# Transposing the third batch's q and k by DMA instead of on TensorE, with two natural buffers shared crosswise

## The chip, the cores and the metric

The kernel runs on one core of one Trainium2 chip. The metric is the device time of one execution in microseconds. Profiles give the span of one execution, which is some 2 us shorter than the time. All runs compared here are of the fast state, except a single run of one experiment (e6), whose state can't be told and which is used for its trace alone. Three slow runs (350.61 and 622.58 us of the kernel before, 390.21 us of e3) are in no ratio.

## The reference

Two stages, both of which the kernel does in one pass. First, attention with a sliding window of 32 to either side, for 8 batches of 8 heads, 576 positions and 64 numbers per position. Then a two-layer network over the 4608 resulting rows of 512.

```
scores = q @ k.T / 8, masked to |i - j| <= 32
x      = softmax(scores) @ v            # reshaped to (4608, 512)
h      = x @ w_in                       # 512 -> 2048
g      = smelu(h)                       # 0, (h + 1)^2 / 4 or h
out    = g @ w_out                      # 2048 -> 512
```

## The kernel before

The network is a loop of 144 steps. A step is one chunk of the first layer: 8 matmuls into `hp`, then ScalarE and VectorE make `gT` of it. 8 matmuls of the second layer, 256 columns wide and written as `op`, or 4 of 512 columns, follow most steps. The attention of batch b+1 is sprinkled between the steps. A table says at which step a piece goes: `scores` (small matmuls of q and k, exp, mask) and `sums` (small matmuls with v and with ones, then the division, into `xT`, which the network reads). Eight steps use 256 rows.

`scores` needs q and k transposed: `qT` and `kT`. The kernel before has two ways to get them:

```python
def load_rows(b, t):                   # long rows: 9 positions in one run
    x = nat.tile([128, NU, 2, D], BF, name=nm, tag=nm)       # two buffers for q, two for k
    ...
    nc.gpsimd.dma_start(out=dst[b], in_=src[b].rearrange("(m e) (p j) d -> (e p) m (j d)", e=2, j=9))

def load_nat(b, t):                    # natural rows: one position is one run
    x = dst[b] = nat.tile([128, NU, 2, D], BF, name=nm, tag=nm)
    for h in range(2): ...

def tpose(...):                        # TensorE: transposes into PSUM, then a copy to qT or kT
    ...
            nc.tensor.transpose(ps[HD[h], j - j0], src[h][:, D * j:D * j + D], ident)
    ...

def xpose(b, t):                       # DMA: one transposing transfer, sync queue
    nc.sync.dma_start_transpose(out=qkT(b, t).rearrange("d (u p) -> d u p", p=128),
                                in_=(qn, kn)[t][b].rearrange("p u h d -> p (u h d)"))
```

Batches 0, 1 and 2 (`LONG = 3`) are loaded in long rows and transposed on TensorE. Batches 3 to 7 are loaded in natural rows and transposed by DMA. All loads but q's first are issued by GpSimd, which runs ahead of the other engines as far as buffers and its DMA completions allow; it casts float32 to bfloat16 on the way. The outputs and the DMA transposes are issued by the sync engine, in program order.

The softmax here doesn't subtract the row's maximum and nothing guards it: scores larger than these inputs give would overflow.

## Time and profile before

| what | value |
|---|---|
| time | 311.72 us, median of 3 (311.7 to 312.26) |
| span of the profile | 310.0 us |
| TensorE matmul busy | 296.7 us (96%) |
| VectorE, ScalarE, GpSimd busy | 79%, 63%, 24% |
| granted TensorE clock | full in all slices |
| DMA transposes | 5 of q, 5 of k |

The busy time of TensorE has its ends modelled, so 96% doesn't mean that it works at its peak. What makes it the bound is that next to nothing is seen to hold it up. One wait in the prediction's list isn't one, as I saw later: `op <- issue`, 4.9 us in 31 pieces of 0.16. It belongs to this group of the costliest lines (busy us, mean ns, then idle before):

```profile
L432 PE MATMUL op<-w_out,gT 128*128 128x512 bf16 x477 | 123.0, 379 | 5.1 <-issue 4.9
```

The program has 512 of these matmuls, as the 512 weight loads of the same line show. 35 records are missing, and each of the 31 gaps is what a missing record leaves. Where all 512 were recorded (the changed kernel, below) the wait is gone. A second trace of that same kernel (e9) lacks 36 again, and the wait is back:

```profile
PE op L431 <- issue: 4.8, 30, 0.2
```

### The profile page before, as it was taken

The numbers are of one execution on the slowest core, as the hardware profiler recorded it, in microseconds if no ns is written. First come the engines' busy times: TensorE is split into PE (matmuls) and PEld (weight loads), VectorE is DVE, ScalarE is ACT, GpSimd is POOL, SyncE is SP. The second block draws the span as 40 slices with busy tenths as digits, with TensorE's granted clock in tenths as the row PEclk, the third lists the DMA queues.
The fourth block names the chain that finished last, engine by engine and source line by source line (L and its number), as shares of the span: only waits on it lengthen the run. The fifth ranks groups of instructions, "written<-read, shape, count | busy, mean of one in ns | idle before, by whom it ended". The sixth has DMA issues, their size and how long they took to land.

```text
span 310.0 us, 8569 instructions
## 1 busy us (share of the span) xinstructions
PE 296.7 (96%) x3669; PEld 206.7 (67%) x3706; DVE 244.7 (79%) x381; ACT 195.3 (63%) x323; POOL 73.8 (24%) x89
## 2 busy tenths in 40 slices
PE   7889999999999999999999999999999999999995
PEld 3467878876666666666666666666666666666652
DVE  3278568988988888898888888888888888888760
ACT  3688786866775666567656666566676666554431
POOL 8897354563036133041404000000000000000000
PEclk9999999999999999999999999999999999999999
DMA  9999999999999999298989391005501100100111
GB/s 153 186 192 197 173 209 184 186 151 170 156 151 170 141 183 172 54 98 176 157 77 94 52 182 43 34 36 113 112 34 36 37 36 34 37 36 34 56 47 68
DMA packets 124118, 34.54 MB, mean 111 GB/s; under 512 B 108208, under 2 KB 119728, under 8 KB 124080
## 3 DMA queue, kind: packets, MB, share of 16 engines
q0 software_dynamic: 94736, 18.06, 76.3%
q1 hardware_dynamic: 29200, 15.63, 21.8%
q8 instruction: 29, 0.48, 0.6%
q10 hardware_dynamic: 144, 0.29, 0.3%
q14 instruction: 9, 0.07, 0.1%
HBM read 36.70 MB, written 9.44 MB: 149 GB/s over the span
## 4 chain that ended last, share of the span: by engine, by line
PE 88%; DMA 4%; POOL 3%; issue 2%; ACT 1%; DVE 0%; POOLq 0%
PE hp L492 39%; PE op L432 35%; PE bb L293 6%; PE op L448 4%; DMA w_in<-in_moe_w_in_dram 4%; PE bb L227 2%; PE tp L187 1%; POOL vn L106 1%; POOL w_in L110 1%; ACT pt L235 1%; POOL kh L85 0%; DVE gT L501 0%; ACT mx L500 0%; PE bb L252 0%; ACT rr L496 0%
## 5 line engine op out<-in xcount | busy, mean ns | idle before, releaser
L492 PE MATMUL hp<-xT,w_in 128*128 128x256 bf16 x1152 | 149.4, 273 | 1.7 <-DMA w_in<-in_moe_w_in_dram 1.1
L496 ACT ACTIVATE rr<-hp 128x512 f32<-128x512 f32 x144 | 85.7, 595 | 87.4 <-PE hp L492 87.2
L492 PEld LDWEIGHTS <-w_in 128*128 128x128 bf16 x1152 | 112.0, 98 | 41.5 <-issue 2.3
L432 PE MATMUL op<-w_out,gT 128*128 128x512 bf16 x477 | 123.0, 379 | 5.1 <-issue 4.9
L503 DVE TENSOR_TENSOR mx<-hp,rr 128x512 f32<-128x512 f32 x137 | 94.5, 690 | 31.1 <-ACT rr L496 29.0
L504 DVE SCALAR_TENSOR_TENSOR gT<-rr,mx 128x512 bf16<-128x512 f32 x137 | 95.2, 695 | 4.7
L432 PEld LDWEIGHTS <-gT 128*128 128x128 bf16 x512 | 47.5, 98 | 36.8
L235 ACT ACTIVATE pt<-bb 128x1024 bf16<-128x1024 f32 (+1 forms) x33 | 32.7, 1002 | 4.4 <-PE bb L227 2.9
L106 POOL DMA_DIRECT2D vn<-in_v_dram x32 | 27.6, 874 | 30.8 <-PE bb L227 28.0
L305 DVE TENSOR_TENSOR xT<-bb,rc 128x512 bf16<-128x512 f32 (+1 forms) x32 | 21.1, 658 | 10.3 <-ACT rc L300 9.8
L437 ACT COPY osb<-op 128x512 f32<-128x512 f32 x32 | 18.6, 582 | 11.6 <-PE op L432 11.1
L300 ACT ACTIVATE rc<-lr 128x512 f32<-128x512 f32 (+2 forms) x40 | 23.5, 588 | 1.3
L98 POOL DMA_DIRECT2D qn<-in_q_dram x10 | 12.2, 1221 | 46.4 <-DMA qT<-qn 40.7
L299 ACT ACTIVATE lr<-bb 128x512 f32<-128x512 f32 (+2 forms) x40 | 22.0, 551 | 0.4 <-PE bb L293 0.4
L201 DVE TENSOR_TENSOR pt<-pt,mask 128x1024 bf16<-128x1024 bf16 (+1 forms) x33 | 20.3, 614 | 0.0
L293 PE MATMUL bb<-pt,ones 64*64 64x256 bf16 (+3 forms) x352 | 19.6, 256 | 0.1
L293 PE MATMUL bb<-pt,vn 64*64 64x128 bf16 (+3 forms) x712 | 18.4, 204 | 0.2 <-DMA vn<-in_v_dram 0.2
L293 PEld LDWEIGHTS <-vn 64*64 64x64 bf16 x712 | 16.7, 107 | 0.4 <-DMA vn<-in_v_dram 0.4
L448 PE MATMUL op<-w_out,gT 128*128 128x256 bf16 x128 | 16.5, 273 | 0.0
L293 PEld LDWEIGHTS <-ones 64*64 64x64 bf16 x352 | 10.2, 105 | 8.6 <-issue 8.6
L98 POOL DMA_DIRECT2D kn<-in_k_dram x10 | 12.1, 1216 | 8.3 <-DMA kn<-in_k_dram 3.7
L227 PE MATMUL bb<-qT,kT 64*64 64x128 bf16 (+1 forms) x520 | 13.1, 217 | 0.3 <-DVE kT L190 0.2
(56 smaller groups left out, 116.9 us busy)
## 6 DMA issues: line engine op xcount, KB each, us to landing
out_dram<-osb SPq DMA_DIRECT2D x36, 256.0 KB, 2.3
vn<-in_v_dram POOLq DMA_DIRECT2D x32, 144.0 KB, 9.7
qn<-in_q_dram POOLq DMA_DIRECT2D x10, 288.0 KB, 7.8
kn<-in_k_dram POOLq DMA_DIRECT2D x10, 288.0 KB, 9.6
w_in<-in_moe_w_in_dram POOLq DMA_DIRECT2D x12, 128.0 KB, 5.5
w_out<-in_moe_w_out_dram POOLq DMA_DIRECT2D x3, 512.0 KB, 15.5
qn<-in_q_dram POOLq DMA_DIRECT2D x2, 576.0 KB, 13.2
kn<-in_k_dram POOLq DMA_DIRECT2D x2, 576.0 KB, 14.5
```

The lines of the kernel that those rows point to most:

```text
L98: nc.gpsimd.dma_start(out=x[:, :, h], in_=src[b, NY * h:NY * h + NY].rearrange("y s d -> (y s) d") .rearrange("(u p) d -> p u d", p=128))
L106: nc.gpsimd.dma_start(out=vn[b][64 * a:64 * a + 64, :, h], in_=v[b, y:y + 2].rearrange("y s d -> (y s) d") .rearrange("(c r) d -> r c d", ...
L235: A.activation(p, ps[:, :, :w * n].rearrange(like, y=m), AF.Exp, scale=D ** -0.5)
L293: nc.tensor.matmul(bb[HD[h], a, o + c0:o + c1], ones[HD[a]] if c is None else vn[b][HD[a], c, h], p(a, h), start=n == 0, stop=True, skip_g ...
L299: A.activation(lr[:, :, :D0], bb[:, :, D0:2 * D0], AF.Ln)
L300: A.activation(rc[:, :, :D0], lr[:, :, :D0], AF.Exp, scale=-1.0)
L432: nc.tensor.matmul(o, gT[tt // 2][:, j, 128 * (tt % 2):128 * (tt % 2) + 128], w_out[:, j], start=not done, stop=len(done) == 2 * NF - 1, s ...
L448: nc.tensor.matmul(o[:, tt], gT[p][:, j, 128 * tt:128 * tt + 128], w_out[:, j, 256 * half:256 * half + 256], start=not done, stop=len(done ...
L492: nc.tensor.matmul(hp[:, j], w_in[:, kk, 256 * f + 128 * j:256 * f + 128 * j + 128], xT[:, kk, r0:r0 + TB], start=n == 0, stop=n == 3)
L496: A.activation(rr, hp, AF.Relu, scale=0.5, bias=0.5)
L503: V.tensor_max(mx, hp, rr)
L504: V.scalar_tensor_tensor(g, rr, 1.0, mx, op0=ALU.min, op1=ALU.mult)
```

## The change

Its intent is to take the transposes of batch 2 off TensorE. Batch 2 is loaded in natural rows and transposed by DMA. The sums and scores around it are set to other steps, so that the first scores of batch 2 come a little later. SBUF use stays what it was, four tiles: two for batch 1's long rows, and two for the natural rows of all later batches. q of batch b takes one of the two and k the other, and in the next batch it's the other way round. So the next q is loaded into the buffer of this k, once this k is transposed.

```diff
-    LONG = 3
+    LONG = 2
     def load_rows(b, t):
-        x = nat.tile([128, NU, 2, D], BF, name=nm, tag=nm)
+        x = nat.tile([128, NU, 2, D], BF, name=nm, tag="long")
     def load_nat(b, t):
-        x = dst[b] = nat.tile([128, NU, 2, D], BF, name=nm, tag=nm)
+        x = dst[b] = nat.tile([128, NU, 2, D], BF, name=nm, tag=f"n{(b + t) % 2}", bufs=1)
-    put([(load_rows, 2, t) for t in range(2)] + [(load_v, 2, n) for n in range(4)])
+    put([(load_nat, 2, t) for t in range(2)] + [(load_v, 2, n) for n in range(4)])
-    for n, a in enumerate((18, 21, 24, 27)):
+    for n, a in enumerate((18, 20, 22, 28)):
         at(a, seq[2 + n][0])                        # sums
-    for n, a in enumerate((18, 21, 25, 27)):
+    for n, a in enumerate((18, 20, 26.5, 28)):
         at(a, seq[3 + n][1])                        # scores; the third is batch 2's first
-    for b, *a in ((1, 11, 12), (2, 19.5, 22.5)):
-        for t in range(2):
-            at(a[t], (tposes, b, (t, 0), (t, 1)))
-    loads, xps = {}, {}
-    for b in range(LONG, B):
+    for t in range(2):
+        at(11 + t, (tposes, 1, (t, 0), (t, 1)))
+    loads, xps = {}, {16: [(2, 0)], 18: [(2, 1)]}
+    for b in range(LONG + 1, B):
         ...
-            xps.setdefault(a + 5 + t, []).append((b, t))
+            xps.setdefault(a + 6 + 2 * t, []).append((b, t))
```

## The prediction

> **What bounds the kernel now.** I began with the head of the page and its slices, to see which engine is full and when.
>
> ```profile
> PE 296.7 (96%) x3669; PEld 206.7 (67%) x3706; DVE 244.7 (79%) x381; ACT 195.3 (63%) x323; POOL 73.8 (24%) x89
> PE   7889999999999999999999999999999999999995
> PEclk9999999999999999999999999999999999999999
> DMA  9999999999999999298989391005501100100111
> ```
>
> TensorE is busy to nine tenths or more in every slice from the fourth to the last but one, at full granted clock. The 16 DMA engines look full as well for the first 16 slices (124 us). Two full resources can't both be the bound, so I asked next what TensorE ever waits for, which the view of waits answers for that engine:
>
> ```profile
> PE op L432 <- issue: 4.9, 31, 0.2
> PE z L336 <- DVE warm L126: 1.2, 1, 1.2
> PE hp L492 <- DMA w_in<-in_moe_w_in_dram: 1.1, 2, 0.6
> PE hp L492 <- DVE xT L305: 0.4, 1, 0.4
> ```
>
> Columns: total us, times, longest us. All waits for DMA together are about 2 us, on w_in at the start and first inputs. The loads that fill the DMA engines afterwards run ahead of their use. So the time after about 23 us is the sum of what TensorE is given to do, and 88% of the chain that ended last lies on TensorE. Work removed from it comes off the time, if no wait grows in its place. The chain around the third batch's transposes shows what there is to remove (start, length, what):
>
> ```profile
> 54.95 0.87 PE op L448 x8
> 55.82 1.12 PE tp L187 x36
> 56.95 0.98 PE hp L492 x8
> 57.93 0.87 PE op L448 x8
> ...
> 62.18 0.87 PE op L448 x8
> 63.06 1.13 PE tp L187 x36
> 64.18 0.98 PE hp L492 x8
> 65.16 0.87 PE op L448 x8
> ```
>
> The tp pieces are the transposes of q and of k of batch 2, and both lie on the chain. The hp piece after each takes 0.98 us where a piece that follows another big matmul takes 0.87: switching into the 128-row matmuls again costs 0.11 us.
>
> **What the Trainium skill says.** "TensorE: Matmul & The Clock Gate", Part 4: PE-mode transpose, gives about 275 ns for a transpose in a kernel's context. The trace has 219 ns for one record, but they overlap: 36 in 1.12 us is 31 ns each on the chain, and that is the number to use. The same section says that the result lands in PSUM and needs a copy. The trace agrees: four copies on ACT of about 0.76 us and four on DVE of about 0.73 us for this batch.
>
> "Advanced Engine Details and Errata", X-Bar Transpose (TRN2), calls transposing DMAs as fast as regular ones, 350 to 400 GB/s. In the trace one transpose (128 x 2304 elements of 2 bytes, 590 KB) holds its queue for 2.8 us when nothing else runs, some 210 GB/s. That is slower than the page, and no more than ordinary traffic reaches here.
>
> "DMA: Bandwidth & Descriptors", Issuing engines are not separate DMA queues, says that transposes from the sync queue share the 16 engines with the loads. The trace agrees. The queue's order of time, with batch 3's pair under full load and batch 4's beside little:
>
> ```profile
> 76.95 6.82 SPq L194 DMA_TRANSPOSE qT<-qn  x1
> 83.93 5.57 SPq L194 DMA_TRANSPOSE kT<-kn  x1
> ...
> 107.83 2.79 SPq L194 DMA_TRANSPOSE qT<-qn  x1
> 110.79 2.41 SPq L194 DMA_TRANSPOSE kT<-kn  x1
> ```
>
> From issue to landing the loaded pair took 12.8 and 7.6 us, against a best of 4.8 and 4.7.
>
> **The change part by part.**
>
> *Removed from TensorE.* 2 groups of 36 transposes: 1.12 + 1.13 = 2.25 us of chain. With each goes one switch, 2 x (0.98 - 0.87) = 0.22 us. Sum 2.47 us, all on the path.
>
> *Removed elsewhere.* Eight copies (about 3.0 us on each of ACT and DVE) and one memset of 0.11 us in the preamble. DVE is at 9.0 of 10 us there, but TensorE waits for it almost nowhere: worth 0 by itself, some room for what follows.
>
> *Loads in natural rows.* The same 1.18 MB of q and k are written in 128-byte pieces instead of 1152-byte ones, 4608 packets instead of 512 for each of the two tensors. "DMA: Bandwidth & Descriptors", Why small descriptors are slow, predicts a loss, and the DMA records show its size: stretches with only 1152-byte packets ran at about 205 KB/us, with only 128-byte packets at about 153. Per tensor that is 590/153 - 590/205 = 3.9 - 2.9, so 1.0 us later for q and 2.0 us for k. GpSimd pays 4 issues of 1.22 us instead of 2 of 0.76, on an engine with little else to do. None of it is on the path.
>
> *DMA transposes added.* q2 and k2 are transposed by the sync queue, placed after steps 16 and 18 (a step is one first-layer chunk of hp, 1.75 us or more; step 16 runs at about 47.3 us). What holds them is the landing of the rows. GpSimd's order of time in the kernel before:
>
> ```profile
> 34.74 0.75 POOL L92 DMA_DIRECT2D qn<-in_q_dram  x1 [1.95 <-DMA qn<-in_q_dram]
> 38.02 0.74 POOL L92 DMA_DIRECT2D kn<-in_k_dram  x1 [2.52 <-DMA kn<-in_k_dram]
> ...
> 45.65 1.22 POOL L98 DMA_DIRECT2D qn<-in_q_dram  x1 [2.32 <-DMA w_out<-in_moe_w_out_dram]
> ```
>
> The DMA view gives 15.6 and 15.5 us to landing for the first two: q2 at 50.3, k2 at 53.5. With the loss above I estimate 51.3 and 55.5. The first transpose starts near 51.5 and lands, if as badly as batch 3's, at 64. The second starts when the queue is free, 51.5 + 6.8 = 58.3, and lands at 58.3 + 7.6 = 66. First use: scores of batch 2, at step 25 (69.1 us) before, moved by the change to after step 26. Before, the second-layer matmuls of step 26 end at about 72.1; less the 2.5 us removed, less the scores of step 25 (0.35) that are not yet done, 69.2. Margin 3 us. It's the thinnest of the new ones.
>
> *The crosswise buffers.* q3 takes the buffer of k2, k3 that of q2. So q3 can't be issued at 45.65 as before but only when kT of batch 2 has landed, about 66: 20 us later. Four issues of 1.22 us, then 6 to 9 us to landing on engines that are by then nearly idle: q3 at about 75, k3 at 79. Its transposes, now after steps 28 and 30 (some 73 to 78 us), then land at about 82 and 88. Their first use, at step 39, is near 95 (97 before). 7 us of margin. For later batches the load of b+1 starts when b's k is transposed, about 6 steps before b's first scores, and must be there 11 steps before its own, 17 or so steps later: 12 steps, over 23 us, for a load that needs about 12. No wait on TensorE.
>
> *Moved.* Attention work of batch 1 goes from steps 21 and 24 to 20 and 22, and batch 2's first scores from 25 to 26.5. The number of switches is the same. Two sums two steps apart are found before at steps 30 and 32, where TensorE loses less than 0.1 us, so I count 0.1 us for new tight spots.
>
> Sum: -2.47 + 0.1 = -2.4 us. 311.72 - 2.4 = 309.3 us.
>
> **The rivals.**
>
> *kT of batch 2 comes late.* For it: full DMA engines from 44 to 60 us, batch 3's pair at 12.8 us, one queue shared with output stores. Against it: I took those bad durations already, and after batch 2's values nothing more is loaded, because q3 is blocked. Were the rows 3 us later still and the transposes no faster, TensorE would stand for 0 to 3 us: 309.5 to 312, no gain. I give it 15%.
>
> *The crosswise wait starves batch 3 or a later one.* For it: loads start 20 us later and prefetch is one batch deep instead of two. Against: the margins of 7 us and more. If a single batch lost 3 us, 312; if all five did, some 320. 4%.
>
> *The saving is hidden anyway,* because DVE (79%) takes over. For it: 9.0 of 10 us between 50 and 60. Against: DVE loses 3.0 us of copies in just that stretch, and itself waits 29 us for ACT in the span. 311; 4%.
>
> *More than the sum is won,* since emptier DMA engines speed up TensorE. Against: in the stretch at 88 us with batch 3's transposes in flight the hp pieces are 0.87 us, as at 280 us with idle DMA. Below 308.5: 2%.
>
> **Range and chances.** The saving is read off the chain and small, 0.8%. The spread of the three runs before is 0.56 us. Below, little can happen: 308.7. Above, a stall at batch 2 of some 1.5 us: 310.8. 2% is 6.2 us; nothing removed can give that, and only the starving of several batches can cost it. Faster by over 2%: 1%; within: 97%; slower: 2%.
>
> **What would show it.** In the changed trace the chain has no tp piece after 40 us. The matmul that followed them takes 0.87 us. Transposed k of batch 2 lands before 67 us, and the first scores of batch 2 start near 69 with no wait on a DMA. GpSimd stands before q3 until the transposes' landing. The DMA slices thin out after 65 us and fill those later. TensorE busy is some 2.5 us less, with its idle time unchanged. Wrong would be a wait of TensorE on kT or qT, or on xT and pt at steps 20 to 30, of more than 1 us.

## The result, and the profile after

The changed kernel takes 309.15 us, median of 4 runs (309.13 to 309.35). The kernel before took 311.99 us in the runs it is compared with (311.70 to 313.73). The ratio is 0.9902, 95% interval 0.9873 to 0.993. Ratios are the mean time of one kernel's fast runs over that of the other's in the same rounds, so they aren't quite the ratio of the medians quoted. The span went from 310.0 to 307.6 us.

The span's difference, 2.46 us, is not a measure of the change. TensorE's last matmul ends 8.81 us after the start of the last step in both traces, but from there to the end of the span the changed kernel takes 3.95 us instead of 3.57: six semaphore waits of the sync engine, some 0.06 us apart, come after the last store has landed instead of before it. The times don't show this: the profiled run's time is 2.1 us above its span before (312.14 us) and 1.8 us above it in the changed kernel (309.35 us).

The head of the page, to be held against that of before:

```profile
PE 300.2 (98%) x3634; PEld 205.0 (67%) x3634; DVE 242.1 (79%) x376; ACT 192.6 (63%) x319; POOL 76.8 (25%) x91
PE   8989999999999999999999999999999999999994
DMA  9999999999999968996899156990910011011101
```

Nothing else took over. DVE and ACT fell by 2.6 and 2.7 us, about what the copies took. PE seems 3.5 us busier with less to do; that is again the missing records, this time present. The group of second-layer matmuls counts all 512 and waits for nothing:

```profile
L431 PE MATMUL op<-w_out,gT 128*128 128x512 bf16 x512 | 130.4, 380 | 0.0
```

So for TensorE a busy total is no measure of 2 us. What is one is the start of each step, read from the records of its first `hp` matmul, of which both traces have all 1152:

| step | before, us | changed, us | difference |
|---|---|---|---|
| 11 | 34.28 | 33.92 | 0.36 |
| 19 | 53.91 | 53.53 | 0.38 |
| 29 | 76.35 | 73.51 | 2.84 |
| 143, the last | 297.65 | 294.81 | 2.84 |

From step 29 on the two kernels are in lockstep to the last step. Up to step 19 the change has done nothing yet; the 0.38 us are scatter of the start, where TensorE waits for the first pieces of w_in among other things (1.1 us in the trace before, 0.4 in the changed one; the 13 traces of this study reach step 11 between 33.7 and 35.4 us). The change itself is worth 2.84 - 0.38 = 2.46 us, all of it between steps 19 and 29. I call that stretch's length the **stretch**: 76.35 - 53.91 = 22.44 us before, 73.51 - 53.53 = 19.98 us changed. It's free of the start's scatter, and it will serve as the measure in the experiments.

The chain that ended last, at the same places as before (start, length, what):

```profile
54.57 0.87 PE op L447 x8
55.44 0.87 PE hp L491 x8
...
62.84 0.87 PE op L447 x8
63.72 0.87 PE hp L491 x8
...
68.06 0.86 PE op L431 x4
68.93 0.35 PE bb L227 x16
69.27 0.98 PE hp L491 x8
```

The two tp pieces are gone and what followed them takes 0.87 us. The bb piece at 68.93 is the first scores of batch 2, with no wait before it. The sync queue shows what it might have waited for (start, time that issuing took):

```profile
50.93 6.75 SPq L194 DMA_TRANSPOSE qT<-qn  x1
57.78 6.34 SPq L194 DMA_TRANSPOSE kT<-kn  x1
...
74.19 6.41 SPq L194 DMA_TRANSPOSE qT<-qn  x1
80.76 6.55 SPq L194 DMA_TRANSPOSE kT<-kn  x1
```

The DMA view gives 13.5 and 8.3 us from issue to landing for the first pair: k transposed is there at 57.78 + 8.3 = 66.1 us, 2.8 us before it is used. GpSimd's order of time shows the crosswise wait, 19 us long, ended by that landing:

```profile
46.84 0.85 POOL L106 DMA_DIRECT2D vn<-in_v_dram  x1 [1.67 <-DMA w_out<-in_moe_w_out_dram]
66.84 2.42 POOL L98 DMA_DIRECT2D qn<-in_q_dram  x2 [19.15 <-DMA kT<-kn]
```

### The profile page after: what moved, and what is told of

The parts are those of the page before. It is cut to its first block, busy times and chain, and to the rows that moved or that the text cites. A ratio compares the mean times of both kernels' runs of the same rounds, so it can differ in the third digit from the quotient of the medians.

```text
span 307.6 us, 8460 instructions
## 1 busy us (share of the span) xinstructions
PE 300.2 (98%) x3634; PEld 205.0 (67%) x3634; DVE 242.1 (79%) x376; ACT 192.6 (63%) x319; POOL 76.8 (25%) x91
## 4 chain that ended last, share of the span: by engine, by line
PE 90%; ACT 3%; DVE 2%; DMA 2%; POOL 1%; issue 1%; POOLq 0%; ACTq 0%
PE hp L491 39%; PE op L431 37%; PE bb L293 6%; PE op L447 4%; PE bb L227 2%; DMA vn<-in_v_dram 2%; ACT pt L235 1%; POOL vn L106 1%; PE tp L187 1%; DVE xT L305 1%; ACT rc L300 1%; ACT lr L299 1%; DVE mx L502 0%; ACT rr L495 0%; POOL kh L85 0%
## 5 line engine op out<-in xcount | busy, mean ns | idle before, releaser
L495 ACT ACTIVATE rr<-hp 128x512 f32<-128x512 f32 x144 | 85.6, 594 | 87.5 <-PE hp L491 87.5
L431 PE MATMUL op<-w_out,gT 128*128 128x512 bf16 x512 | 130.4, 380 | 0.0
L98 POOL DMA_DIRECT2D qn<-in_q_dram x12 | 14.6, 1223 | 113.0 <-DMA kT<-kn 109.3
L300 ACT ACTIVATE rc<-lr 128x512 f32<-128x512 f32 (+2 forms) x40 | 23.5, 587 | 1.3
L293 PEld LDWEIGHTS <-vn 64*64 64x64 bf16 x712 | 16.7, 107 | 0.4 <-DMA vn<-in_v_dram 0.4
L293 PEld LDWEIGHTS <-ones 64*64 64x64 bf16 x352 | 10.3, 105 | 8.7 <-issue 8.6
L98 POOL DMA_DIRECT2D kn<-in_k_dram x12 | 14.6, 1235 | 0.6 <-DMA vn<-in_v_dram 0.3
```

The source lines that it names most:

```text
L98: nc.gpsimd.dma_start(out=x[:, :, h], in_=src[b, NY * h:NY * h + NY].rearrange("y s d -> (y s) d") .rearrange("(u p) d -> p u d", p=128))
L293: nc.tensor.matmul(bb[HD[h], a, o + c0:o + c1], ones[HD[a]] if c is None else vn[b][HD[a], c, h], p(a, h), start=n == 0, stop=True, skip_g ...
L300: A.activation(rc[:, :, :D0], lr[:, :, :D0], AF.Exp, scale=-1.0)
L431: nc.tensor.matmul(o, gT[tt // 2][:, j, 128 * (tt % 2):128 * (tt % 2) + 128], w_out[:, j], start=not done, stop=len(done) == 2 * NF - 1, s ...
L495: A.activation(rr, hp, AF.Relu, scale=0.5, bias=0.5)
```

## The experiments

The theory: the saving is the time of 72 transposes on TensorE and of the two switches around them, nothing else, and it holds as long as k transposed lands before its scores. Rivals: the new steps save something themselves; the copies on ScalarE and VectorE were part of the price; the crosswise buffers, or the shape of the loads, help or hurt. The record marks the result of every kernel as right, that of e6 too, which is wrong on purpose: batch 2's q and k stand at wrong positions in it. The numbers of q and k are so small in this reference (0.1 times normal ones) that the softmax comes out nearly uniform, so the comparison hardly sees which q meets which k. That e1 to e11 pass it says little about their transposes.

| run | median us | ratio to before (95%) | stretch us |
|---|---|---|---|
| before | 311.99 | 1 | 22.44 |
| changed | 309.15 | 0.9902 (0.9873 to 0.993) | 19.98 |
| e1, old steps | 309.40 | 0.9917 (0.9904 to 0.993) | 19.98 |
| e2, new steps alone | 312.75 | 1.0026 (1.0018 to 1.0035) | 23.28 |
| e3, transposes back | 312.28 | 1.0009 (1.0 to 1.0018) | 22.44 |
| e4, and the copies | 312.68 | 1.0029 (1.002 to 1.0039) | 22.99 |
| e5, own buffers | 313.42 | 1.0041 (1.0026 to 1.0057) | 23.09 |
| e6, long rows (wrong on purpose) | 309.13, one run | none | 19.97 |
| e7, scores early | 317.15 | 1.0163 (1.0142 to 1.0184) | 27.06 |
| e8, joined | 309.40 | 0.9912 (0.9894 to 0.9929) | 19.76 |
| e9, changed again | 309.37 | 0.9906 (0.9877 to 0.9935) | 19.98 |
| e10, joined again | 309.44 | 0.992 (0.9893 to 0.9948) | 19.76 |
| e11, batch 1 too | 328.45 | 1.0514 (1.0475 to 1.0552) | 19.98 |

The kernel before had medians of 311.96 to 312.04 us in these calls.

### e1: the changed kernel at the old steps

```diff
-    for n, a in enumerate((18, 20, 22, 28)):
+    for n, a in enumerate((18, 21, 24, 27)):
-    for n, a in enumerate((18, 20, 26.5, 28)):
+    for n, a in enumerate((18, 21, 25, 27)):
```

> The changed kernel, but the sums and scores of batches 1 and 2 stay at their old steps (18, 21, 24, 27 and 18, 21, 25, 27). Theory (the saving is TensorE's 72 transposes alone, and the new steps are only there to give the transposed k time): in the changed kernel step 25 starts at 65.29 us and k transposed of batch 2 landed at 66.1 us, so the scores, called about 66.2, just make it; 309.1 to 309.7 us, with at most 0.5 us of TensorE waiting at the first scores of batch 2. Rival (the new steps themselves save time): the gain shrinks visibly, over 310 us, without a wait on the transpose.

The stretch is the changed kernel's to the hundredth. The new steps save nothing. k transposed landed at 57.85 + 8.1 = 65.95 us (the DMA view), and the chain has the first scores directly behind the matmuls before them:

```profile
65.41 0.87 PE hp L491 x8
66.28 0.35 PE bb L227 x16
```

So they made it by 0.3 us in this trace. The new steps turn 0.3 us of margin into 2.8: insurance, not gain.

### e2: the new steps alone

```diff
-    for n, a in enumerate((18, 21, 24, 27)):       # sums
+    for n, a in enumerate((18, 20, 22, 28)):
-    for n, a in enumerate((18, 21, 25, 27)):       # scores
+    for n, a in enumerate((18, 20, 26.5, 28)):
-    for b, *a in ((1, 11, 12), (2, 19.5, 22.5)):   # TensorE's transposes
+    for b, *a in ((1, 11, 12), (2, 19.5, 23.5)):
```

> The kernel before with the new steps alone (sums 18, 20, 22, 28; scores 18, 20, 26.5, 28), batch 2 still in long rows and transposed by TensorE; its k at step 23.5 instead of 22.5, because at 22.5 it would want the PSUM tile of the sums of step 22, whose last reader comes later. Theory: the steps are worth nothing, 311.6 to 312.0 us, the time of before. Rival (part of the gain comes from the steps): under 311.

Neither: it's slower than before, by 0.84 us of stretch. TensorE's waits have a new line, and the chain there runs over VectorE:

```profile
PE bb L293 <- DVE qT L190: 0.8, 1, 0.8
```

```profile
57.14 1.28 DVE qT L190 x2
58.42 0.04 issue
58.46 0.60 PE bb L293 x18
```

The transposes at step 19.5 take both PSUM tiles that scores and sums use. The sums at step 20 have to wait until the last copy has emptied one. At the old steps the sums came at 21 and didn't meet it. My expectation that the steps are worth nothing holds only where no transposes stand beside them.

### e3 and e4: the transposes back, without and with their copies

The same `extra` is placed at steps 19.5 and 23.5 in both; e3 leaves out the last line.

```diff
+    def extra(b, t):
+        x = (qn, kn)[t][b]
+        todo = []
+        for half, pool in ((0, ps_s), (1, ps_n)):
+            tp = pool.tile([128, 2, 8, 128], BF, name="tp", tag="bb")
+            for part, (j0, j1) in enumerate(((0, 5), (5, 9))):
+                for j in range(j0, j1):
+                    for h in range(2):
+                        nc.tensor.transpose(tp[HD[h], part, j - j0], x[:, 9 * half + j, h], ident)
+                todo.append(((A.copy, V.tensor_copy)[part], tp[:, part, :j1 - j0], part, j1 - j0))
+        for copy, ps, part, n in todo:
+            copy(scratch[part][:, :n], ps)          # e4 only
```

> The changed kernel plus 72 TensorE transposes of batch 2's q and k, at steps 19.5 and 23.5, into PSUM tiles that nobody reads; no copies. Result unchanged. Theory: the saving is TensorE's time alone, so it comes back whole, +2.47 us: 311.6 us. Rival (the eight copies on ScalarE and VectorE carried part of the cost): clearly less than +2.4, say 310.5.

> As e3, and the eight copies of before (four 128x640 on ScalarE, four 128x512 on VectorE, out of PSUM) go to a scratch tile. Theory: the copies add nothing, within 0.2 us of e3, 311.6. Rival: over 0.5 us more than e3.

e3's stretch is 22.44 us, that of before, and 2.46 us more than the changed kernel's. The whole price is back with TensorE's part alone:

```profile
55.83 1.13 PE tp L341 x36
56.95 0.98 PE hp L509 x8
```

Its median of 312.28 us lies 0.7 above what I expected, and 0.3 above before's of the same rounds. Its fast runs spread from 311.56 to 313.3. The start of its trace was late: step 19 at 53.92 us, as in the trace before (53.91), against 53.53 in the changed kernel.

e4 is 0.55 us of stretch dearer than e3 (0.4 us in the medians), which is about the limit I had set for the rival. But it isn't engine time that is paid:

```profile
PE bb L295 <- DVE scratch L346: 0.5, 1, 0.5
```

That is the wait of e2 again. The copies hold the PSUM tile past step 20. In the kernel before, with the sums at 21, that wait doesn't occur, so there the copies cost nothing; at the new steps they would cost half a microsecond.

### e5: own buffers instead of the crosswise pair

```diff
-        x = dst[b] = nat.tile([128, NU, 2, D], BF, name=nm, tag=f"n{(b + t) % 2}", bufs=1)
+        x = dst[b] = nat.tile([128, NU, 2, D], BF, name=nm, tag=f"n{t}", bufs=2)
```

> The changed kernel with two natural buffers each for q and for k (four instead of two, 9.2 KB more of every partition), so the next q waits for no transpose of this k. Theory (the crosswise wait costs nothing, because the loads have slack both ways): the time of the changed kernel, 309.1 to 309.5 us; the third batch's successor is loaded from about 50 us on instead of 66.8, and the transposes of batch 2 run beside it. Theory's finer part: they already run beside the rest of batch 2's own loads, so k transposed lands at 66 to 68 us, still before 68.9. Rival A (the sharing holds the time up): faster than 308.9. Rival B (the wait protects the transposes from the loads): k lands after 69, TensorE waits 1 to 3 us, 310 to 312.

My theory fell here, and rival B is right, with a median above its range. Twenty fast runs lie between 311.8 and 315.1 us: the kernel with more buffers loses the whole gain and more. They fall into two groups: eleven with a mean granted clock of 0.998 or 0.999 took 311.8 to 313.43 us, nine with 0.989 to 0.994 took 313.5 to 315.13. So in nine of them the stand of TensorE seems to have cost clock as well, as it does in e7; the profiled run is of the first group. TensorE's longest wait, and the chain before it:

```profile
PE bb L227 <- DMA kT<-kn: 3.0, 1, 3.0
```

```profile
58.31 14.04 DMA kT<-kn
72.35 0.04 issue
72.40 0.42 PE bb L227 x16
```

The transpose of k was issued 0.5 us later than in the changed kernel (58.31 against 57.78), but took 14.0 us to land instead of 8.3. GpSimd, which no longer waits, had put batch 3's loads beside it:

```profile
50.34 2.43 POOL L98 DMA_DIRECT2D qn<-in_q_dram  x2 [1.46 <-DMA qn<-in_q_dram]
```

In the 14 us from issue to landing GpSimd's queue moved 6733 packets beside the 4229 of the sync queue. In the changed kernel's 8.3 us it was 1332 beside 4272: the rest of batch 2's own loads ran out, and then the engines had only transposes and stores. The two lines of each view, e5 first:

```profile
q0 software_dynamic: 6733, 0.86, 118.2%
q1 hardware_dynamic: 4229, 1.18, 64.7%
```

```profile
q1 hardware_dynamic: 4272, 1.21, 107.5%
q0 software_dynamic: 1332, 0.17, 33.5%
```

So the wait for the buffer is what makes the transpose of batch 2's k fast enough. It costs TensorE nothing, and it holds back loads that nobody needs yet.

### e6: the same traffic with long rows, wrong on purpose

```diff
-    put([(load_nat, 2, t) for t in range(2)] + [(load_v, 2, n) for n in range(4)])
+    put([(load_rows_wrong, 2, t) for t in range(2)] + [(load_v, 2, n) for n in range(4)])
     # load_rows_wrong: long rows into the natural tiles, then transposed as if natural
```

> The changed kernel, but batch 2's q and k are loaded in long rows (1152-byte pieces) into the same tiles and then transposed by DMA as if they lay in natural rows: the numbers of batch 2 come out wrong on purpose, the traffic is what matters. Theory: q lands 1.0 us and k 2.0 us earlier than in the changed kernel (50.9 and 55.0 there), k transposed about 1 to 2 us earlier than 66.1; the time is the same, 309.2, since nothing waits for it. Rival (the shape of the loads matters for the time): over 0.5 us of change.

q landed at 33.56 + 15.9 = 49.5 us and k at 36.49 + 15.9 = 52.4, against 36.33 + 14.5 = 50.8 and 39.36 + 15.5 = 54.9 in the changed kernel: 1.3 and 2.5 us earlier (the prediction had worked out 1.0 and 2.0). One trace can't tell 2.5 from 2.0: in the changed kernel's second trace (e9) k landed 1.1 us later, at 39.65 + 16.3 = 55.95. k transposed landed at 57.60 + 6.3 = 63.9, 2.2 us earlier. The stretch is the same within 0.01 us. In these traces the natural rows cost margin and no time.

### e7: the first scores of batch 2 too early

```diff
-    for n, a in enumerate((18, 20, 26.5, 28)):
+    for n, a in enumerate((18, 20, 22, 28)):
```

> The changed kernel with the first scores of batch 2 at step 22, beside the sums there, instead of 26.5. Theory: the scores are then called at 60.9 us, k transposed lands at 66.1; TensorE stands for 5.2 us there, less one switch of 0.11: 314.2 us. Rival (there is more slack than the trace says, or the wait is absorbed later): under 312.

The wait is as expected, 5.5 us for 5.2. The time is 3 us worse than expected. Busy time by stretch shows why: the figure of 0.71 or 0.56 behind POOL's is the granted clock.

```profile
61.00:66.80 5.80, 0.34 (x28) 0.22 (x20) 1.64 (x3) 0.55 (x1) 0.00 (x0) 0.71 1.39 175
66.80:70.80 4.00, 3.94 (x35) 2.91 (x36) 1.25 (x2) 1.96 (x4) 3.27 (x3) 0.56 0.48 31
70.80:75.00 4.20, 4.20 (x33) 3.01 (x31) 2.88 (x5) 2.35 (x4) 4.20 (x6) 1.00 2.32 143
```

While TensorE stood, its clock was taken down, and the next 4 us ran at little more than half. The chain has these pieces:

```profile
66.86 0.64 PE bb L227 x14
67.50 1.82 PE op L447 x8
69.33 1.40 PE hp L491 x8
```

In full clock they take 0.23, 0.98 and 0.87 us, so 1.78 us more. 5.5 + 1.78 less 0.22 for the joined excursion (see e8) is 7.06, and the stretch grew by 27.06 - 19.98 = 7.08. The Trainium skill, "TensorE: Matmul & The Clock Gate", What's actually happening, says that the clock falls to half after an idle window of about 3.4 us and comes back after as much busy time. The way back agrees: a mean of 0.56 over the 4.0 us is what half the clock until 70.3 us gives, 3.4 us after the first scores. The fall doesn't: a mean of 0.71 over the 5.8 us is what full clock until 63.4 us and half from there give, and TensorE's last matmul had ended at 61.3, so only 2.1 us had been idle. In the profiled run of e5 a stand of 3.0 us left the clock at 1.00. So the length of a stand alone doesn't tell here whether the clock falls; what does isn't shown.

### e8, e9 and e10: one excursion fewer

e8 and e10 are one kernel; e9 is the changed kernel again, as control of e10.

```diff
-    for n, a in enumerate((18, 20, 22, 28)):      # sums: the third moves beside batch 2's first scores
+    for n, a in enumerate((18, 20, 26.5, 28)):
```

> The changed kernel with the last sums of batch 1 moved from step 22 to 26.5, so that they stand beside batch 2's first scores: one switch of TensorE between small and large matmuls fewer. Theory (a switch costs 0.11 us of the chain): from step 19 to step 29 0.11 us less than the changed kernel's 19.98 us, the time 309.05 us, which the timing can hardly tell from 309.15. Rival (what followed a switch was the price of the transposes, not of switching): no change of that stretch.

> The changed kernel once more, as the control of e10 on the same chip in the same rounds: 309.1 to 309.5 us, ratio 0.991. From step 19 to step 29 it takes 19.98 us in its trace, whatever the start does.

> e8's kernel (the last sums of batch 1 beside batch 2's first scores) against the control of the same rounds. In e8 the stretch from step 19 to 29 took 19.76 us instead of 19.98, but its start was in the later of two variants (step 5 at 24.48 us, against 23.74 in the changed kernel), which hid it. Theory (an excursion of TensorE to small matmuls costs 0.12 us going in and 0.11 coming back, and the rest is the start's scatter): 0.2 us under the control in the median, and again 19.76 us in the stretch. Rival (the joined sums give the gain back later): no difference.

Both traces of the joined kernel have a stretch of 19.76 us, 0.22 less than that of both traces of the changed one. Twice what I had expected in e8, because the way into small matmuls costs as well:

```profile
67.85 0.86 PE op L431 x4
68.71 0.42 PE bb L293 x28
69.13 0.23 PE bb L227 x16
69.35 0.98 PE hp L491 x8
```

The scores alone, after a large matmul, took 0.35 us; behind the sums they take 0.23. An excursion of TensorE costs 0.12 us in and 0.11 back. The Trainium skill, "TensorEngine Tiling (Array Packing)", Key Properties, says that changing the tiling mode drains TensorE, which fits these pieces; that draining is the cause isn't shown by a run.

In the timing no gain is seen: 309.44 us for e10 (9 runs, 308.99 to 312.11) against 309.37 for e9 (4 runs, 309.24 to 309.95). 0.2 us is less than the scatter, and whether the joined kernel is faster in time stays open.

### e11: batch 1 too

```diff
-    LONG = 2
+    LONG = 1
-    put([...] + [(load_rows, 1, t) for t in range(2)])
+    put([...] + [(load_nat, 1, t) for t in range(2)])
-    for t in range(2):
-        at(11 + t, (tposes, 1, (t, 0), (t, 1)))
-    loads, xps = {}, {16: [(2, 0)], 18: [(2, 1)]}
+    loads, xps = {}, {9: [(1, 0)], 10: [(1, 1)], 16: [(2, 0)], 18: [(2, 1)]}
```

> The changed kernel with batch 1 treated like batch 2: natural rows, DMA transposes after steps 9 and 10, no TensorE transposes left but batch 0's. It removes another 2.5 us of TensorE. Theory (the technique pays only where the transposed k can land before its scores): rows land near 35 and 39 us, the transposes run one after the other beside full load, k transposed lands between 50 and 56 us, but its scores are called at about 38 us: TensorE stands 12 to 18 us, and after such a stand the clock is low for a while (e7: 1.5 us more); 309.2 - 2.5 + 12 to 18 + 1.5 = 320 to 326 us. Rival (later work absorbs it): under 315.

The direction is as expected, and the size is above the range: TensorE stood for 20 us, not 12 to 18.

```profile
PE bb L227 <- DMA kT<-kn: 20.0, 1, 20.0
```

k's transpose was issued at 43.81 us but took 16.7 us to land, beside loads of v and above all of w_out (1.07 MB in 2534 packets on GpSimd's queue). It landed at 60.5 us, where I had expected 50 to 56. Batch 1's scores were called at 40.5 us. With the loads in this order, the technique ends with batch 2; another order wasn't tried.

## Why the prediction was right or wrong

The time was predicted at 309.3 us and measured at 309.15, within the range of 308.7 to 310.8. That it came so close is partly luck: the kernel before took 311.99 us in the compared runs and not 311.72, and the medians differ by 2.84 us and not by 2.4; 0.38 us of that, in the traces, is the start. Step by step:

- **TensorE bounds the kernel, and work taken from it comes off the time.** Right. From step 29 to the last the lead stays at 2.84 us. e3 puts the work back and gets the old stretch.
- **2.25 us of transposes and 0.22 us of switches.** Right: 2.47 predicted, 2.46 measured between steps 19 and 29. The rest of the difference of the traces, 0.38 us, is scatter of the start.
- **Copies and memset worth 0.** Right for the kernel before. e4 adds that it depends on the steps: beside the new ones, the copies would hold a PSUM tile for half a microsecond too long.
- **Natural rows land 1.0 and 2.0 us later.** The mechanism was right, and the size within the scatter of single traces: e6 shows 1.3 and 2.5.
- **k of batch 2 lands transposed at 66, scores at 69.2, margin 3.** Measured 66.1, 68.93 and 2.8.
- **The crosswise wait: q3 loaded at 66 instead of 45.65.** It was issued at 66.84. I counted this as a delay with enough margin. It is also what makes the margin at batch 2, which e5 showed. The prediction had said that nothing more is loaded because q3 is blocked, but used it only as an argument against a late k. Without the wait the prediction's first rival, late k, is what happens.
- **Batch 3's transposes land at 82 and 88 with 7 us of margin.** Mis-sized. They landed at 74.19 + 13.3 = 87.5 and 80.76 + 10.3 = 91.1, and the first scores came at 94.7: 3.6 us of margin. The loads weren't the reason, they landed at 74.0 and 79.1 us where 75 and 79 had been said. The failed step is the time given to the transposes, on engines said to be "by then nearly idle". The DMA engines were nearly idle for a short while only: the time that packets took, as a share of the 16 engines' time (it can exceed 1, as packets overlap), was 0.77 from 66 to 70 us, against 2.98 before the change, and 2.2 to 2.5 from 70 to 82, when batch 3's own k and v were loaded. So the first of the two transposes took as long as batch 2's first, 13.3 us for 13.5.
- **0.1 us for new tight spots.** There were none: no wait of TensorE between 50 and 80 us. The 0.1 us is too small to be told from the timing.
- **DVE doesn't take over; emptier DMA engines don't speed up TensorE.** Both right: the last 114 step lengths (from start to start) agree to 0.01 us, while the DMA rows of the two pages differ.
- **TensorE busy 2.5 us less, its idle time unchanged.** This sign didn't come: busy went up by 3.5 us, as the trace before lacked 35 records. The prediction listed the wait on issue, 4.9 us, and didn't ask what it was.

## What to carry to other kernels

On a kernel bound by one engine, read the gain of taking work from it off the chain, switches of mode included, and verify it on the starts of the loop's steps, not on busy totals. Then ask when the replacement's result lands, beside which traffic: a transposing DMA of 590 KB took 5 us with little beside it and up to 17 us beside loads. A buffer shared so that the next load has to wait can be worth more than another buffer, because it keeps loads that nobody needs yet off the engines while something urgent moves.

## What the Trainium skill lacked or had wrong

- "TensorE: Matmul & The Clock Gate", Part 4: PE-mode transpose, gives about 275 ns for one transpose. Transposes of 128 x 64 blocks into the two halves of the output's partitions overlapped here: 219 ns in each record, but 36 in 1.12 us of the chain.
- "TensorEngine Tiling (Array Packing)", Key Properties, has the drain at a change of mode but no figure. Here an excursion from 128-row matmuls to 64-row ones cost 0.12 us going in and 0.11 us coming back.
- "Advanced Engine Details and Errata", X-Bar Transpose (TRN2), calls transposing DMAs as fast as regular ones, at 350 to 400 GB/s. One of 590 KB held its queue for 2.8 us with little beside it, some 210 GB/s. From issue to landing it took 4.8 us so, 14.0 us beside loads in 128-byte packets (e5), and 16.7 us beside loads of v and w_out, 420 bytes to a packet on average (e11). No page gives a figure for that.
- "TensorE: Matmul & The Clock Gate", What's actually happening, has the clock fall after an idle window of about 3.4 us. In e7 it fell 2.1 us after TensorE's last matmul.
- No page that I read says that missing matmul records look like waits: 35 missing ones showed as 31 pieces of "issue", 4.9 us in all, and made TensorE look 7.4 us less busy in that group (123.0 us for 477 records, 130.4 for 512).
